# A state-space layer followed by a two-product MLP: the second product accumulated tile by tile, and the engine order written out by hand

## The chip, the cores and the metric

The kernel runs on one core of a Trainium2 chip. The metric is device time in microseconds (us), the median of several executions. One execution was recorded by the hardware profiler; its view is called the profile, and its rows the trace. The engines are PE (TensorE, with PEld for its weight loads), DVE (VectorE), ACT (ScalarE), POOL (GpSimd) and SP (SyncE, which here only issues DMAs).

## The reference

```python
# SSD part: batch 4, heads H=8, seq 768, head_dim 32, state 16; float32
cum   = cumsum(log(clip(a, 1e-6, 1)))                 # within a chunk
M     = (C @ B.T) * exp(cum_i - cum_j) * (i >= j)     # per head
y     = M @ x + exp(cum) * (C @ state)
state = exp(sum) * state + (B * exp(cum_last - cum)).T @ x
# MLP part: 3072 tokens, d_model 256, d_ff 2048; w_in and w_out arrive as float64
X = y.transpose(0, 2, 1, 3).reshape(3072, 256)
h = X @ w_in
g = maximum(h, 0) + alpha * minimum(h, 0)
out = g @ w_out
```

## The kernel before, in words

The sequence is cut into 24 chunks of Q = 128 tokens, and two chunks make a pair: 12 pairs, three to a batch element. Two pairs make a group of GT = 512 tokens, so there are NG = 6 groups of the MLP. The hidden width 2048 is NF = 16 tiles of 128.

`load_pair` fetches one pair's B and C (`nat`), x (`xt`), the decays in the layout of the states (`ap`), and the decays of all heads copied to every partition (`abc`, two transfers of 512 KB). `load_rows` and `rows_prep` make the products of the decays from a token to its chunk's end (`prt`) for two batch elements at a time.

`pair(gp)` does the SSD part of one pair. DVE scans `ap` to running products `pf` (L246, L249). POOL clips `abc` (L255), and DVE scans it, with an identity for each head (`ident_h`) as the added term, to the decay matrices `dec` (L258, 1024 elements a partition and chunk). PE transposes `nat` (L267); ACT copies B (`bh`, L271) and makes four masked copies of C (`cz`, L274); DVE makes `cd` (L276). POOL weights B (`bn`, L283), PE multiplies it with x (L290), and DVE masks the product and updates the state (`dm`, `state`, L292 and L302). PE forms the Gram matrices (L312), DVE multiplies them into `dec` (L317), PE sums state part and chunk part into `y` (L325, L332), and ACT copies `y` into the group's transposed input `xT` (L338).

`load_weights` brings a piece of a float64 weight (512 KB: two hidden tiles) as pairs of 32-bit words and builds float32 from them: on ACT `wt` and `wg` (L159, L164), on DVE a clip (L160), the sign, a shift with an exclusive or (L173), and an add (L176). The sign is taken by POOL for `w_in` (L167, 512 elements) and by DVE for `w_out` (L171, two of 256). There are eight pieces of each weight.

`hidden(g, q, t0, nt)` makes four hidden tiles: for each, PE sums two products into `hp` (L352; every float32 product is two matmul instructions in the trace, so four a tile), ACT scales by alpha (L355) and DVE takes the maximum (`gt`, L356). `hp` has two buffers (`ps_h`). `output(g)` then makes the second product: for each 128 tokens, 16 products summed into one `po` (L366, 32 instructions), a DVE copy (L368) and a store for each two.

The last lines set the program order: pair 0; then for group 0 the first 256 tokens with the pieces of `w_in`, and the last 256 with those of `w_out`, pairs 1 to 3 between; `output(0)`; then for each further group four calls of `hidden`, before two of which a pair of the next group is called, and `output(g)`. This is not the order in which the engines work: on every engine the order is set by a planner, which places each instruction by the times that it expects, and takes the program's order as priority. Within an engine's queue the planned order is then strict. Tiles from a pool of n buffers wait for the release of the tile n before.

Of the kernel before, what the change touches and what calls it, by code (L numbers as in the profile page):

```python
# [22 lines left out]
def kernel(  # L23
# [18 lines left out]
    nc = tc.nc  # L42

# [16 lines left out]
    FQ = 4  # L60
    WQ = 256
    assert H * N == P and HD == d_model and KC == 2 and R == CPB == 6
    assert NCH % GC == 0 and GT == 512 and NF % FQ == 0 and d_model <= WQ
# [5 lines left out]
    wld = ctx.enter_context(tc.tile_pool(name="wld", bufs=4))  # L69
    wtp = ctx.enter_context(tc.tile_pool(name="wtp", bufs=2))  # L70
    lda = ctx.enter_context(tc.tile_pool(name="lda", bufs=2))
# [3 lines left out]
    gp = ctx.enter_context(tc.tile_pool(name="gp", bufs=5))  # L75
# [14 lines left out]
    def load_pair(gp):  # L90
        b, c = divmod(2 * gp, CPB)
        sl = slice(c * Q, (c + 2) * Q)
        nat = ldx.tile([P, 2, 2, H * N], F32, name="nat")
        abc = lda.tile([P, 2, H * Q], F32, name="abc")
# [4 lines left out]
                                              ap=[[S, H], [0, N], [1, 2 * Q]]))  # L99
        for k in range(2):  # L100
# [5 lines left out]
        for k in range(2):  # L106
            ts = slice((c + k) * Q, (c + k + 1) * Q)
            first = a[b, 0:1, ts]
            nc.sync.dma_start(
                out=abc[:, k].rearrange("p (h t) -> p h t", h=H),  # L110
                in_=bass.AP(tensor=first.tensor, offset=first.offset, ap=[[0, P], [S, H], [1, Q]]),
            )
        for k in range(2):
            ts = slice((c + k) * Q, (c + k + 1) * Q)
            nc.sync.dma_start(out=xt[:, k].rearrange("p (h d) -> p h d", h=H),
                              in_=x[b, :, ts, :].rearrange("h p d -> p h d"))
# [19 lines left out]

    def load_weights(dst, src, sg):

        d = dst.bitcast(U32)
        if src.dtype == F32:
            nc.sync.dma_start(out=dst, in_=src)
            for i in range(2 if sg else 0):
# [3 lines left out]
        raw = wld.tile([P, 2, WQ, 2], U32, name="raw")  # L148
        nc.sync.dma_start(out=raw.rearrange("p k w t -> p k (w t)"), in_=src.bitcast(U32))
        hi = raw[:, :, :, 1]  # L150
        half = raw.rearrange("p k w t -> p k (w t)").bitcast(U16)
        half = half.rearrange("p k (w t) -> p k w t", t=4)[:, :, :, 1]
        t = wtp.tile([P, 2, WQ], U32, name="wt")
        r = wtp.tile([P, 2, WQ], U32, name="wr")
        g = wtp.tile([P, 2, WQ], F32, name="wg")
        tf = t.bitcast(F32)


        nc.scalar.activation(out=tf, in_=hi.bitcast(F32), func=ACTF.Abs, scale=0.125)  # L159
        nc.vector.tensor_scalar(out=tf, in0=tf, scalar1=F64_INF, scalar2=F64_ZERO,  # L160
                                op0=ALU.min, op1=ALU.max)


        nc.scalar.activation(out=g, in_=half, func=ACTF.Copy,  # L164
                             scale=2.0**-11, bias=2.0**25)
        if sg is None:
            nc.gpsimd.tensor_scalar(out=r, in0=hi.bitcast(F32), scalar1=0.0, scalar2=2.0**31,  # L167
                                    op0=ALU.is_lt, op1=ALU.mult)
        else:
            for i in range(2):  # L170
                nc.vector.tensor_scalar(out=r[:, i], in0=hi[:, i], scalar1=SIGN, scalar2=sg[i],  # L171
                                        op0=ALU.bitwise_and, op1=ALU.bitwise_xor)
        nc.vector.scalar_tensor_tensor(out=r, in0=t, scalar=3, in1=r,  # L173
# [8 lines left out]
    for h in range(H):  # L182
        nc.scalar.copy(out=ident_h[:, h * Q : (h + 1) * Q], in_=ident)
# [35 lines left out]
    prt = {}  # L219

    def rows_prep(i):
# [4 lines left out]
                                op0=ALU.max, op1=ALU.min)  # L226
        nc.vector.memset(d0[:, Q:], 0.0)
# [10 lines left out]
    def pair(gp):  # L238
# [3 lines left out]
        last = c + 2 == CPB  # L242


        pf = work.tile([P, 2 * Q], F32, name="pf")
        nc.vector.tensor_scalar(out=ap, in0=ap, scalar1=1e-6, scalar2=1.0, op0=ALU.max, op1=ALU.min)  # L246
        for k in range(2):
            ks = slice(k * Q, (k + 1) * Q)
            nc.vector.tensor_tensor_scan(out=pf[:, ks], data0=ap[:, ks], data1=zeros, initial=1.0,  # L249
                                         op0=ALU.mult, op1=ALU.add)  # L250


# [180 lines left out]
```

## Time and profile before

| | |
|---|---|
| median of 3 runs | 472.55 us (472.06 to 475.72) |
| the profiled execution's own time | 473.27 us |
| its span in the profile | 471.6 us |
| PE busy | 426.3 us, 1867 matmul instructions |
| DVE busy | 233.2 us |
| ACT busy | 120.1 us |
| POOL busy | 62.9 us |
| bytes moved by DMA | 32.38 MB |

Span and busy times come from the profiled execution; its own time is 1.67 us above its span, and 0.72 us above the median. A busy time is the time in which at least one instruction of the engine ran. The end of a matmul in the trace is modelled, so that PE counts as busy while it crawls at a low clock.

### The profile page before, as it was taken

The numbers are of one execution on the slowest core, as the hardware profiler recorded it, in microseconds if no ns is written. First come the engines' busy times: TensorE is split into PE (matmuls) and PEld (weight loads), VectorE is DVE, ScalarE is ACT, GpSimd is POOL, SyncE is SP. The second block draws the span as 40 slices with busy tenths as digits, with TensorE's granted clock in tenths as the row PEclk, the third lists the DMA queues.
The fourth block names the chain that finished last, engine by engine and source line by source line (L and its number), as shares of the span: only waits on it lengthen the run. The fifth ranks groups of instructions, "written<-read, shape, count | busy, mean of one in ns | idle before, by whom it ended". The sixth has DMA issues, their size and how long they took to land.

```text
span 471.6 us, 4815 instructions
## 1 busy us (share of the span) xinstructions
PE 426.3 (90%) x1867; PEld 271.4 (58%) x1867; DVE 233.2 (49%) x363; ACT 120.1 (25%) x225; POOL 62.9 (13%) x78
## 2 busy tenths in 40 slices
PE   1788679999989799998989998989999999999996
PEld 0345346658844358843448853448864458833785
DVE  2998779899584830065840065840043530034200
ACT  4135437610033220033330023330024320034100
POOL 3554450303401010011010000000000000000000
PEclk9868889999999999999999999999999999999999
DMA  9995668935643430034330030000000000000000
GB/s 166 229 200 201 154 169 188 197 53 136 181 78 90 56 89 1 22 64 105 45 90 1 23 56 12 1 0 0 24 22 0 1 0 24 0 22 1 0 22 22
DMA packets 109365, 32.38 MB, mean 69 GB/s; under 512 B 75856, under 2 KB 105248, under 8 KB 109344
## 3 DMA queue, kind: packets, MB, share of 16 engines
q1 hardware_dynamic: 105184, 31.83, 29.3%
q10 hardware_dynamic: 4160, 0.26, 0.6%
q8 instruction: 14, 0.23, 0.2%
q14 instruction: 7, 0.06, 0.0%
HBM read 28.94 MB, written 3.15 MB: 68 GB/s over the span
## 4 chain that ended last, share of the span: by engine, by line
PE 66%; DVE 15%; issue 9%; ACT 3%; DMA 3%; POOL 2%; SPq 0%; DVEq 0%; POOLq 0%; ACTq 0%
PE po L366 31%; PE hp L352 28%; DVE dec L258 5%; DVE gt L356 3%; PE ss L332 2%; DVE dec L317 2%; POOL wr L167 2%; PE ss L325 1%; DVE pf L249 1%; PE ss L312 1%; ACT gt L355 1%; ACT cz L274 1%; DMA ap<-in_a_dram 1%; PE ss L290 1%; DMA abc<-in_a_dram 1%
## 5 line engine op out<-in xcount | busy, mean ns | idle before, releaser
L352 PE MATMUL hp<-xT,w_in 128*128 128x512 f32 (+1 forms) x448 | 184.9, 560 | 20.1 <-DVE gt L356 18.1
L366 PE MATMUL po<-w_out,gt 128*128 128x256 f32 x768 | 168.9, 380 | 0.2 <-DVE o_sb L368 0.2
L366 PEld LDWEIGHTS po<-w_out,gt 128*128 128x128 f32 x768 | 145.6, 190 | 23.0 <-issue 3.0
L352 PEld LDWEIGHTS hp<-xT,w_in 128*128 128x128 f32 x448 | 81.9, 197 | 112.8 <-DVE gt L356 52.4
L356 DVE SCALAR_TENSOR_TENSOR gt<-hp,s_mul,gt 128x512 f32<-128x512 f32 (+1 forms) x112 | 74.2, 670 | 79.8 <-ACT gt L355 79.4
L355 ACT ACTIVATE gt<-hp,s_alpha 128x512 f32<-128x512 f32 (+1 forms) x112 | 70.0, 627 | 146.6 <-PE hp L352 146.4
L368 DVE COPY o_sb<-po 128x256 f32<-128x256 f32 x24 | 10.2, 423 | 124.6 <-PE po L366 124.6
L258 DVE TENSOR_TENSOR_SCAN dec<-abc,ident_h 128x1024 f32<-128x1024 f32 x24 | 55.4, 2331 | 3.3 <-PE ss L332 3.3
L255 POOL TENSOR_SCALAR abc<-abc 128x1024 f32<-128x1024 f32 x24 | 30.3, 1261 | 112.2 <-DMA abc<-in_a_dram 81.4
L312 PE MATMUL ss<-cz,bh 64*128 64x512 f32 x96 | 33.5, 695 | 6.1 <-DVE cd L276 4.1
L271 ACT COPY bh<-ss 128x256 f32<-128x256 f32 x12 | 4.4, 370 | 105.9 <-PE ss L267 105.9
L317 DVE TENSOR_TENSOR dec<-ss,dec 128x512 f32<-128x512 f32 x48 | 30.5, 680 | 0.6 <-PE ss L312 0.6
L283 POOL TENSOR_TENSOR bn<-nat,prt 128x256 f32<-128x256 f32 x12 | 10.4, 871 | 103.9 <-PE ss L290 56.7
L312 PEld LDWEIGHTS ss<-cz,bh 64*128 64x128 f32 x96 | 10.3, 203 | 22.7 <-ACT cz L274 7.7
L167 POOL TENSOR_SCALAR wr<-raw 128x512 uint32<-128x512 f32 x8 | 17.4, 2192 | 16.6 <-DVE w_in L176 12.9
L274 ACT ACTIVATE cz<-ss,par 128x256 f32<-128x256 f32 x48 | 19.4, 485 | 0.0
L332 PE MATMUL ss<-dec,xt 128*32 128x128 f32 x384 | 17.0, 292 | 2.2 <-DVE dec L317 2.2
L338 ACT COPY xT<-ss 128x512 f32<-128x512 f32 x12 | 7.0, 586 | 44.9 <-PE ss L332 44.9
L173 DVE SCALAR_TENSOR_TENSOR wr<-wt,wr 128x512 uint32<-128x512 uint32 x16 | 12.5, 787 | 5.0 <-POOL wr L167 5.0
L159 ACT ACTIVATE wt<-raw 128x512 f32<-128x512 f32 x16 | 10.7, 675 | 15.9 <-DMA raw<-in_moe_w_in_dram 10.9
L290 PE MATMUL ss<-xt,bn 128*128 128x256 f32 x40 | 12.0, 417 | 2.6 <-POOL abc L257 2.6
L332 PEld LDWEIGHTS ss<-dec,xt 128*32 128x32 f32 x384 | 9.6, 113 | 8.1 <-DVE dec L317 4.3
(46 smaller groups left out, 129.8 us busy)
## 6 DMA issues: line engine op xcount, KB each, us to landing
abc<-in_a_dram SPq DMA_DIRECT2D x24, 512.0 KB, 5.6
raw<-in_moe_w_in_dram SPq DMA_DIRECT2D x8, 512.0 KB, 6.1
raw<-in_moe_w_out_dram SPq DMA_DIRECT2D x8, 512.0 KB, 4.1
xt<-in_x_dram SPq DMA_DIRECT2D x24, 128.0 KB, 4.6
out_dram<-o_sb SPq DMA_DIRECT2D x12, 256.0 KB, 2.1
ap<-in_a_dram SPq DMA_DIRECT2D x12, 128.0 KB
nat<-in_B_dram SPq DMA_DIRECT2D x22, 64.0 KB, 2.8
nat<-in_C_dram SPq DMA_DIRECT2D x22, 64.0 KB, 2.7
```

Source lines behind the costliest of these rows:

```text
L167: nc.gpsimd.tensor_scalar(out=r, in0=hi.bitcast(F32), scalar1=0.0, scalar2=2.0**31, op0=ALU.is_lt, op1=ALU.mult)
L255: nc.gpsimd.tensor_scalar(out=abc[:, k], in0=abc[:, k], scalar1=1.0, scalar2=1e-6, op0=ALU.min, op1=ALU.max)
L258: nc.vector.tensor_tensor_scan(out=dec[:, k].rearrange("p h t -> p (h t)"), data0=abc[:, k], data1=ident_h, initial=0.0, op0=ALU.mult, op1 ...
L274: nc.scalar.mul(cz[:, e].rearrange("p k t -> p (k t)"), ct, par[:, e : e + 1])
L290: nc.tensor.matmul(dps[:, k * HD : (k + 1) * HD], bn[:, k], xt[:, k], start=True, stop=True)
L312: nc.tensor.matmul(gram[r].rearrange("p h t -> p (h t)"), bh[rs, k], cz[rs, :, k], start=True, stop=True, tile_position=(64 * r, 0), skip_ ...
L317: nc.vector.tensor_tensor(out=dec[:, k, hs], in0=gram[r], in1=dec[:, k, hs], op=ALU.mult)
L332: nc.tensor.matmul(y[32 * q : 32 * q + 32, w, k], xt[:, k, h * D : (h + 1) * D], dec[:, k, h], start=False, stop=True, tile_position=(0, 3 ...
L352: nc.tensor.matmul(hp, w_in[:, k, f * P : (f + 1) * P], xts[g][:, k, t0 : t0 + nt], start=(k == 0), stop=(k == KC - 1))
L355: nc.scalar.mul(gt, hp, s_alpha[:, f : f + 1])
L356: nc.vector.scalar_tensor_tensor(out=gt, in0=hp, scalar=s_mul[:, f : f + 1], in1=gt, op0=ALU.mult, op1=ALU.max)
L366: nc.tensor.matmul(po[:, :d_model], gts[g, f // FQ][:, f % FQ, ts], w_out[:, f], start=(f == 0), stop=(f == NF - 1))
```

## The change

The order of PE, DVE and ACT is now the program's order, instruction by instruction (`manual_schedule`); POOL and the DMA queues are still placed by the planner. With this, six things change:

- `hidden(g, f, ...)` makes one hidden tile, and `output(g, f)` adds that tile's share to all four 128-token blocks of the group at once, in two `po` tiles of 512 columns (8 matmul instructions of 256 columns). It follows the first product by LAG = 2 tiles. ACT, not DVE, copies `po` out (two copies of 512 columns a group).
- `pair` is a generator of six stages: loads, `bn`, `pf`, transposes and `cz`; the scan of the first chunk; the scan of the second, states; Gram matrices of the first chunk; of the second; `y`. In groups 1 to 4 the stages of a pair are called ahead of tiles 0, 1, 2, 3, 4 and 6 of each eight. In group 0 two tables (`first`, `second`) give the places.
- For pairs 0 and 1 `abc` isn't loaded: PE spreads the clipped rows (`firsts[0]`) over the partitions, by a product with a column of the identity, into PSUM, 512 columns at a time, and DVE scans from there. The buffers of `abc` are now three single chunks.
- The conversion of weights is cut in two: `convert_a` on ACT, `convert` on DVE. The sign of `w_in` is taken by DVE in one instruction, not by POOL. Transfers run six pieces ahead (`wld` has 6 buffers), the ACT part two pieces and the DVE part one piece ahead of the tiles that use them.
- The first transfers are put in the order pair 0, two weight pieces, pair 1, four pieces, pair 2.
- `ident_h` is made by one DVE copy instead of eight on ACT.

```diff
+    ctx.enter_context(tc.manual_schedule(engines={
+        mybir.EngineType.PE, mybir.EngineType.DVE, mybir.EngineType.Activation}))
...
+    LAG = 2
+    NB = 2
...
-    wld = ctx.enter_context(tc.tile_pool(name="wld", bufs=4))
+    wld = ctx.enter_context(tc.tile_pool(name="wld", bufs=6))
...
-    gp = ctx.enter_context(tc.tile_pool(name="gp", bufs=5))
+    gp = ctx.enter_context(tc.tile_pool(name="gp", bufs=16))
...
+        for k in range(2 if gp >= NB else 0):
+            t = lda.tile([P, H * Q], F32, name="abc")
...
+    def convert_a(dst, src, sg):
...
+        nc.scalar.activation(out=t.bitcast(F32), in_=hi.bitcast(F32), func=ACTF.Abs, scale=0.125)
+        nc.scalar.activation(out=g, in_=half, func=ACTF.Copy, scale=2.0**-11, bias=2.0**25)
...
         if sg is None:
-            nc.gpsimd.tensor_scalar(out=r, in0=hi.bitcast(F32), scalar1=0.0, scalar2=2.0**31,
-                                    op0=ALU.is_lt, op1=ALU.mult)
+            nc.vector.tensor_single_scalar(out=r, in_=hi, scalar=SIGN, op=ALU.bitwise_and)
...
+        for k in range(2):
+            if abc:
+                nc.vector.tensor_tensor_scan(out=dv[:, k], data0=abc[k], data1=ident_h,
+                                             initial=0.0, op0=ALU.mult, op1=ALU.add)
+            for w in range(0 if abc else 2):
+                t = ps_s.tile([P, 512], F32, name="ss")
+                for q in range(4):
+                    row = (b % 2 * H + 4 * w + q) * CPB + c + k
+                    nc.tensor.matmul(t[:, q * Q : (q + 1) * Q],
+                                     ident[:RW, row : row + 1].to_broadcast([RW, P]), firsts[0],
+                                     start=(q == 0), stop=True, skip_group_check=True)
+                nc.vector.tensor_tensor_scan(out=dv[:, k, ws], data0=t, data1=ident_h[:, ws],
+                                             initial=0.0, op0=ALU.mult, op1=ALU.add)
...
+    def output(g, f):
+
+        if f == 0:
+            pos[g] = [ps_o.tile([P, 2, d_model], F32, name="po") for i in range(GC // 2)]
+        gt = gts.pop((g, f))
+        for t in range(GC):
+            nc.tensor.matmul(pos[g][t // 2][:, t % 2], gt[:, t * Q : (t + 1) * Q], w_out[:, f],
+                             start=(f == 0 and t % 2 == 0), stop=(f == NF - 1),
+                             skip_group_check=True)
+        if f == NF - 1:
+            for i, po in enumerate(pos.pop(g)):
+                o_sb = op.tile([P, 2, d_model], F32, name="o_sb")
+                nc.scalar.copy(out=o_sb, in_=po)
...
+    pieces = in_pieces + out_pieces
+    for i in range(2):
+        load_weights(*pieces[i])
+    load_pair(1)
+    for i in range(2, 6):
+        load_weights(*pieces[i])
+    ssm(0, 5)
+    convert_a(*pieces[0])
+    convert(*pieces[0])
+    convert_a(*pieces[1])
     ssm(0)
+    load_pair(2)
+
+    first = {2: (1, 1), 3: (1, 1), 4: (1, 1), 6: (1, 1), 8: (1, 1), 10: (1, 1),
+             11: (2, 1), 12: (2, 1), 13: (2, 1), 15: (2, 1)}
+    second = {1: (2, 1), 3: (2, 1), 4: (3, 1), 6: (3, 1), 7: (3, 1), 9: (3, 1), 11: (3, 1), 13: (3, 1)}
+    for n in range(2):
+        for f in range(NF):
+            i = (n * NF + f) // 2
...
+            if f in (first, second)[n]:
+                ssm(*(first, second)[n][f])
+            hidden(0, f, n * 2 * Q, 2 * Q)
+            if f % 2 == 0 and i + 6 < len(pieces):
+                load_weights(*pieces[i + 6])
+            if f % 2 == 1 and i + 1 < len(pieces):
+                convert(*pieces[i + 1])
+                if i + 2 < len(pieces):
+                    convert_a(*pieces[i + 2])
+            if n and f >= LAG:
+                output(0, f - LAG)
+    for i in range(NF * (NG - 1) + LAG):
+        g, f = divmod(NF + i, NF)
+        nxt = 2 * g + 2 + f // 8
...
+        if f % 8 in (0, 1, 2, 3, 4, 6) and nxt < NP:
+            ssm(nxt)
+        if g < NG:
+            hidden(g, f, 0, GT)
+        output(*divmod(NF + i - LAG, NF))
```

More of the change, by code (lines that the diff above doesn't have):

```diff
@@ L181 @@
     ident_h = const.tile([P, H * Q], F32, name="ident_h")
-    for h in range(H):
-        nc.scalar.copy(out=ident_h[:, h * Q : (h + 1) * Q], in_=ident)
+    nc.vector.tensor_copy(out=ident_h.rearrange("p (h t) -> p h t", h=H),
+                          in_=ident.unsqueeze(1).to_broadcast([P, H, Q]))
     bmask = const.tile([P, HD], F32, name="bmask")
@@ L219 @@
     prt = {}
+    firsts = {}
     def rows_prep(i):
@@ L396 @@
-    output(0)
-    for g in range(1, NG):
-        for q in range(NQ):
-            if g + 1 < NG and q % 2 == 0:
-                ssm((g + 1) * GC // 2 + q // 2)
-            hidden(g, q, 0, GT)
-        output(g)
+            gts[g, f] = gp.tile([P, GT], F32, name="gt")
+        hp = ps_h.tile([P, GT], F32, name="hp")[:, :nt]
+        for k in range(KC):
+            nc.tensor.matmul(hp, w_in[:, k, f * P : (f + 1) * P], xts[g][:, k, t0 : t0 + nt],
+                             start=(k == 0), stop=(k == KC - 1))
```

171 lines of the change are left out of this document (82 added, 89 removed).

## The prediction, written before the changed kernel ran

> **What bounds the kernel now.** I read the page first: PE is busy 90% of the span and holds 66% of the chain that ended last, so what counts is where PE waits, and where it is busy without being at its rate.
>
> ```profile
> span 471.6 us, 4815 instructions
> ...
> PE 426.3 (90%) x1867; PEld 271.4 (58%) x1867; DVE 233.2 (49%) x363; ACT 120.1 (25%) x225; POOL 62.9 (13%) x78
> ...
> PEclk9868889999999999999999999999999999999999
> ...
> PE 66%; DVE 15%; issue 9%; ACT 3%; DMA 3%; POOL 2%; SPq 0%; DVEq 0%; POOLq 0%; ACTq 0%
> ```
>
> In the clock's row each digit is a slice of 11.8 us; in slices 2 to 6 it falls to 6 to 8 tenths. So I cut the span into stages (columns: length, then busy time and instructions of PE, PEld, DVE, ACT and POOL, the granted clock, the share of DMA and its rate).
>
> ```profile
> 0.00:30.00 30.00, 14.85 (x64) 7.78 (x64) 19.70 (x34) 9.62 (x24) 16.10 (x23) 0.88 0.94 194
> ...
> 30.00:72.00 42.00, 31.88 (x121) 17.97 (x120) 32.70 (x58) 18.82 (x37) 19.01 (x15) 0.80 0.66 177
> ...
> 72.00:122.00 50.00, 48.56 (x257) 35.90 (x258) 48.32 (x84) 17.76 (x37) 11.50 (x13) 1.00 0.69 151
> ...
> 122.00:174.00 52.00, 46.50 (x207) 24.13 (x207) 31.62 (x44) 15.05 (x27) 7.88 (x14) 1.00 0.43 96
> ...
> 201.60:246.00 44.40, 39.63 (x174) 17.87 (x173) 29.89 (x41) 15.05 (x27) 7.12 (x12) 1.00 0.40 80
> ...
> 344.80:384.30 39.50, 39.01 (x176) 17.97 (x175) 19.61 (x31) 15.04 (x27) 0.00 (x0) 1.00 0.02 7
> ```
>
> Up to 122 us DVE is the fuller engine (19.7 of 30, 32.7 of 42, 48.3 of 50), while PE lacks 15.2, 10.1 and 1.4 us of these stages, at a clock of 0.88, 0.80 and 1.00. From 122 on PE leads, but loses 5.5 us (122 to 174) and 4.8 (201.6 to 246) in the stages that hold pairs with their scans; where the last pairs run (344.8) it loses 0.5. The waits name the cause:
>
> ```profile
> PE hp L352 <- DVE gt L356: 18.1, 9, 4.1
> ...
> DVE wr L173 <- POOL wr L167: 5.0, 4, 1.9
> ```
>
> Two things, then: an opening bound by DVE and its partners, and DVE's scans that hold back `gt`, whose release the next `hp` needs. The rates of undisturbed PE come from the chain in order of time (start, length, what):
>
> ```profile
> 344.84 0.44 PE ss L267 x4
> ...
> 345.28 0.87 PE ss L290 x4
> ...
> 350.02 1.16 PE ss L325 x8
> ...
> 351.18 1.06 PE ss L332 x32
> ...
> 411.96 28.27 PE hp L352 x64
> ...
> 440.23 27.64 PE po L366 x128
> ...
> 467.90 0.42 DVE o_sb L368
> ```
>
> The second product, 128 instructions of 256 columns, takes 27.64 us: 0.216 each, without a gap. The first, 64 of 512 columns, takes 28.27, 0.442 each, where twice 0.216 would be 0.432: it waits a little for `gt` at every tile. A pair costs PE 0.44 (transposes), 0.87 (L290), 1.16 (L325), 1.06 (L332) and the Gram row, 1.99:
>
> ```profile
> 347.79 1.99 PE L312 MATMUL ss<-cz,bh 64*128 64x512 f32 x8
> ```
>
> together 5.52 us.
>
> **The change, groups 1 to 5.** A tile is 4 x 0.432 + 8 x 0.216 = 3.46 us of PE, and 80 tiles 276.4. Eight pairs (4 to 11) lie among them: 44.2. Two tiles of the lagging second product: 3.5. One transpose of decays: 0.4. Sum **324.5 us** if nothing waits. Does anything? The rows by form (busy us, mean ns; then idle before):
>
> ```profile
> L352 PE MATMUL hp<-xT,w_in 128*128 128x256 f32 x128 | 39.3, 448 | 9.9 <-DVE gt L356 7.9 <-DVE w_in L176 2.0
> ...
> L356 DVE SCALAR_TENSOR_TENSOR gt<-hp,s_mul,gt 128x512 f32<-128x512 f32 x80 | 59.3, 747 | 74.4 <-ACT gt L355 74.4
> ...
> L356 DVE SCALAR_TENSOR_TENSOR gt<-hp,s_mul,gt 128x256 f32<-128x256 f32 x32 | 14.9, 476 | 5.4 <-ACT gt L355 5.0
> ...
> L355 ACT ACTIVATE gt<-hp,s_alpha 128x512 f32<-128x512 f32 x80 | 55.0, 687 | 122.8 <-PE hp L352 122.8
> ...
> L355 ACT ACTIVATE gt<-hp,s_alpha 128x256 f32<-128x256 f32 x32 | 15.1, 476 | 23.8 <-PE hp L352 23.6
> ...
> L258 DVE TENSOR_TENSOR_SCAN dec<-abc,ident_h 128x1024 f32<-128x1024 f32 x24 | 55.4, 2331 | 3.3 <-PE ss L332 3.3
> ...
> L368 DVE COPY o_sb<-po 128x256 f32<-128x256 f32 x24 | 10.2, 423 | 124.6 <-PE po L366 124.6
> ...
> L160 DVE TENSOR_SCALAR wt<-wt 128x512 f32<-128x512 f32 x16 | 7.2, 467 | 0.0
> ...
> L171 DVE TENSOR_SCALAR wr<-raw,s_out 128x256 uint32<-128x256 uint32 x16 | 5.8, 395 | 0.0
> ...
> L173 DVE SCALAR_TENSOR_TENSOR wr<-wt,wr 128x512 uint32<-128x512 uint32 x16 | 12.5, 787 | 5.0 <-POOL wr L167 5.0
> ...
> L176 DVE CUSTOM_DVE_ANT_0 w_in<-wr,wg 128x1024 uint16<-128x1024 uint16 x8 | 6.8, 876 | 0.0
> ...
> L176 DVE CUSTOM_DVE_ANT_0 w_out<-wr,wg 128x1024 uint16<-128x1024 uint16 x8 | 5.6, 699 | 0.0
> ```
>
> After the first product of a tile come ACT 0.69 and DVE 0.75; the buffer of `hp` is wanted again only after two shares of the second product and one first product, 5.2 us, and `gt` itself 6.9 us later. In the worst stage DVE's queue holds one scan (2.33), a mask and two state updates (estimated from rows of their sizes, L173's 0.68 and two of L356's 0.48: 1.64) ahead of `gt`: 4.0 + 0.75 is done inside 5.2. ACT's `cz` stands ahead of one scaling only. Before, two scans stood back to back, and the buffer was wanted 1.73 us after. So the wait of 18.1 us should go. What is late next is PE itself. Bounds: 324.5, and 341 if each of the eight pairs still cost the 2.0 us that the nine waits of L352 average (16). ACT's two copies of `po` (1.2 to 1.4 us by L338 below and L355) stand between the last share of a group and the first of the next; there the first product of tile 2, 1.73 us, covers them. The 10.2 us of L368 leave DVE, where nobody waited for them except at the end. SP's queue gets a store behind each `po` copy; the loads behind it are those of a pair wanted eight tiles, 27 us, later.
>
> **The opening to the first tile.**
>
> ```profile
> 4.07 0.42 PE L267 MATMUL ss<-ident,nat 128*128 128x128 f32 x1
> ...
> 9.09 0.48 PE L267 MATMUL ss<-ident,nat 128*128 128x128 f32 x1 [1.66 <-DMA nat<-in_C_dram]
> ...
> 24.74 0.58 ACT L338 COPY xT<-ss 128x512 f32<-128x512 f32 x1 [1.17 <-PE ss L332]
> ...
> 26.89 1.63 POOL L283 TENSOR_TENSOR bn<-nat,prt 128x256 f32<-128x256 f32 x1
> ...
> 28.02 1.06 DVE L173 SCALAR_TENSOR_TENSOR wr<-wt,wr 128x512 uint32<-128x512 uint32 x1
> ...
> 29.93 0.68 DVE L173 SCALAR_TENSOR_TENSOR wr<-wt,wr 128x512 uint32<-128x512 uint32 x1
> ...
> 30.26 4.14 PE L352 MATMUL hp<-xT,w_in 128*128 128x256 f32 x8
> ```
>
> Before, the last transpose of pair 0 waits for its load until 9.09, `y` is copied at 24.74, and the first hidden matmul starts at 30.26, when DVE has converted a piece. Now 1 MB of `abc` is gone from the first transfers:
>
> ```profile
> abc<-in_a_dram SPq DMA_DIRECT2D x24, 512.0 KB, 5.6
> ```
>
> I put the transposes at 7 (bounds 4.5, where they would wait for the decays' transposes, and 9.1). Then 0.6 for them, one spread of four heads, eight matmuls of 128 columns like the eight of L325 (1.16), the pair's DVE work, and a conversion. DVE's pair: 233.2 in all, less 74.2 (both L356 forms), 10.2 (L368), 7.2 + 5.8 + 12.5 + 6.8 + 5.6 (conversions), is 110.9, over 12 pairs **9.2**. The half scans are taken as halves of L258 (1.17 each; PSUM as source isn't in the trace for a scan: bounds 1.1 and 1.5), the other seven spreads lie beside them. A conversion: L160 0.45, L173 0.68 undisturbed (29.93), L176 0.70, the sign 0.6 (one of 512 elements, between L160's 0.45 and two of L171, 0.72): **2.45**; by the means of the rows it would be 2.74, the upper bound. Sum 7 + 0.6 + 1.2 + 9.2 + 2.45 = 20.4, of which the `ap` part runs while `nat` is awaited: **20 us**. `ident_h` on DVE (two L160, 0.9, up to one L258, 2.3) and the rows' extra clip fall into the wait for loads; without it they would cost themselves.
>
> L173 took 1.06 us at 28.02, beside POOL's L283 of 26.89 to 28.52, and 0.68 alone. The Trainium skill (SBUF — State Buffer, "Who interferes with whom") says that a VectorE instruction with two SBUF inputs contends with a GpSimd instruction that reads SBUF; by that page every conversion would shed what POOL cost it, and the trace agrees in these two rows. Were the 1.06 kept, the first half below would be 8 x 0.38 = 3.0 us longer; its only POOL work now is `bn` and pair 2's clips, so I take 0.68.
>
> **First half of group 0** (16 tiles of 256 tokens, eight pieces of `w_in`, pair 1, and pair 2 to its first Gram stage). DVE: 16 x 0.466 + 8 x 2.45 + 9.2 + 7.9 = 44.1. Each tile's matmuls wait for their conversion, and DVE then waits for matmul and ACT unless a stage stands between. Four instructions of the 256-column row take 4 x 0.307 = 1.23 at the clock of this stage, ACT 0.47. Tiles 0, 10 and 14 have no DVE stage ahead: 1.8 each; 2, 6 and 8 are covered by 1.1 to 1.3: 0.6 each; three odd tiles wait 0.76 for their matmul: 9.5. Sum **53.6 us**. DVE's order here is strict: behind a conversion that waits for its words stand `gt`, and so `hp`, and PE. The words: pair 0, six pieces and pair 1 are 4.4 MB, at the 194 GB/s of the first row 23 us, and piece 5 is wanted at about 43.
>
> **Second half**: PE 16 x 0.864 + 14 x 1.73 = 38.0, pair 3 5.5, the rest of pair 2 3.2, and 1.3 while conversion and `gt` of the turn pass: **48 us**. DVE has 16 x 0.466 + 7 x 2.55 + 10.5 = 35.8, so it follows. **End**: before 3.7 us from the last matmul; now the second ACT copy, 0.58 to 0.69, for 0.42: **4**.
>
> 20 + 53.6 + 48 + 324.5 + 4 = 450.1 us of span, and 1.67 around it: 451.8 against 473.27. The median of the runs was 0.72 lower, so **451**. A check by place: groups 0 and 1 were done at 201.6, where the fifth stage above begins; now at 121.6 + 55.3 + 11 + 3.5 = 191.4. About 10 us come from the opening and 11 from later scans.
>
> **Rivals.** (1) *The clock.* PE is busy some 27 of 54 us in the first half, less than the 31.9 of 42 at which the clock row shows 0.80. At half clock the 1.23 becomes 1.73, in nine places: 4.5 us, **456**; PE's work would still fit beneath DVE's. The Trainium skill (TensorE: Matmul & The Clock Gate, "Part 1") says that about 3.4 us without PE work put the array back to half rate; by that page this rival is to be expected, while the trace shows 0.80 with idle times up to 4 us. (2) *The opening gains nothing*: the stages' hops between PE, ACT and DVE show, and it lasts 132 instead of 121.6: **462**. (3) *Fixed order loses, slower*: in the first 120 us DVE stands for each chain in turn, with nothing pulled ahead. A piece then costs 2.45 + 1.23 + 0.47 + 2 x 0.47 = 5.1, eight 41; pairs 1 and 2 each take what pair 0 took from 4.07 to 24.74 alone, 20: the first half 81, the second 62 with pair 3 bared, and the whole 494. It decides from an opening of 144 us on; the tables, which put DVE stages between conversion and `gt` at ten of 16 tiles, speak against it. (4) *Order without effect*: POOL and the queues are still planned, and loads planned late stop a strict DVE; what is won is waited away, **472**. (5) *Better*: few bare hops and conversions at 2.2: 438.
>
> **How the numbers follow.** Forecast 0.58 (445 to 460), clock 0.08, no gain in the opening 0.10, slower 0.10, no effect 0.07, better 0.07. One per cent, 4.7 us, is about what a measurement can tell from no change. Faster: 0.58 + 0.08 + 0.10 + 0.07 = 0.83; within 0.07; slower 0.10. The range 438 to 468 leaves out the slower, the no-effect and part of the better case; it holds the main stage's upper bound (341) with the rest as forecast.
>
> **What would show it.** The first hidden matmul near 20 us; DVE near full and PE half idle to about 74; from about 122 PE without a gap, chain pieces of L352 and L366 alternating at 1.73; no wait of `hp` for `gt` there; busy PE near 405 us. The prediction is wrong if DVE in the first half waits for DMA or PE more than 10 us in all, or if a pair in groups 1 to 4 costs over 6 us above its 27.6 us of tiles.

## The result, and the profile after

The changed kernel takes 456.27 us (median of 4 runs, 455.88 to 456.93) against 473.96 for the kernel before (four runs here, 472.06 to 475.72): a ratio of 0.9629, 95% interval 0.958 to 0.9678. It is 17.7 us faster; 451 was forecast, in a range of 438 to 468. Lines of the changed kernel have other numbers: the first product is L396, ACT's scaling L399, DVE's maximum L400, the second product L409.

The page of the kernel after, with the rows that answer to those of before:

```profile
span 455.2 us, 4968 instructions
...
PE 421.7 (93%) x1931; PEld 284.0 (62%) x1931; DVE 230.6 (51%) x354; ACT 124.3 (27%) x229; POOL 35.1 (8%) x62
...
PEclk9959787999999999999999999999999999999999
...
PE 86%; DVE 9%; DMA 1%; ACT 1%; issue 1%; ACTq 0%; DVEq 0%
```

PE's share of the chain rose from 66 to 86%, POOL's work fell from 62.9 to 35.1 us, and from the eighth slice on the clock stays at nine tenths or more. The span cut at the forecast's own stages (columns as before: length, busy time and instructions of PE, PEld, DVE, ACT, POOL, granted clock, DMA share, rate):

```profile
0.00:22.10 22.10, 13.11 (x87) 9.34 (x87) 14.55 (x32) 5.90 (x11) 3.67 (x12) 1.00 0.94 210
22.10:78.30 56.20, 36.81 (x162) 26.00 (x163) 39.58 (x68) 19.00 (x40) 8.13 (x13) 0.76 0.70 163
78.30:126.40 48.10, 47.29 (x275) 38.42 (x274) 36.89 (x74) 18.77 (x38) 3.25 (x5) 1.00 0.28 64
126.40:451.50 325.10, 324.53 (x1412) 210.23 (x1410) 139.61 (x182) 80.01 (x139) 20.10 (x32) 1.00 0.17 40
451.50:455.20 3.70, 0.00 (x0) 0.00 (x0) 0.00 (x0) 0.59 (x1) 0.00 (x0) 1.00 0.42 142
```

From 126.4 to 451.5 PE is idle for 0.6 us in 325: nothing is left there but PE's work. Nearly all the waiting is ahead of 78.3. In the stage from 22.1 to 78.3 neither PE (36.8 of 56.2) nor DVE (39.6) is full. PE's waits over the whole run (us in total, times, longest):

```profile
PE hp L396 <- DVE w_in L195: 21.3, 8, 5.3
...
PE hp L396 <- DVE gt L400: 0.8, 1, 0.8
```

The 18.1 us of waits of `hp` for `gt` are 0.8 now. In their place stand 21.3 us in which the first product waits for the conversion of its weights, at eight places, one for each piece of `w_in`. What DVE does in that stage is seen by its own waits from 22.1 to 78.3:

```profile
DVE gt L400 <- ACT gt L399: 13.2, 10, 2.7
DVE dec L322 <- PE ss L318: 1.1, 2, 0.7
DVE dec L361 <- PE ss L356: 1.0, 1, 1.0
```

So the two engines wait in turn. One turn, in the trace by time (start, length, engine, what, idle before and who ended it):

```profile
72.45 0.69 DVE L195 CUSTOM_DVE_ANT_0 w_in<-wr,wg 128x1024 uint16<-128x1024 uint16 x1
...
73.19 2.07 PE L396 MATMUL hp<-xT,w_in 128*128 128x256 f32 x4 [5.28 <-DVE w_in L195]
...
75.31 0.47 ACT L399 ACTIVATE gt<-hp,s_alpha 128x256 f32<-128x256 f32 x1 [5.77 <-PE hp L396]
75.81 0.48 DVE L400 SCALAR_TENSOR_TENSOR gt<-hp,s_mul,gt 128x256 f32<-128x256 f32 x1 [2.67 <-ACT gt L399]
```

PE had stood 5.28 us for this conversion; then DVE, whose next instruction in the fixed order is this tile's maximum, stands 2.67 us while matmul and scaling pass. Of this the four matmul instructions take 2.07 us; at 57.20, in the same stage, four of the same size take 1.13. The granted clock is 0.50 over the first and 1.00 over the second, so the low clock is part of this turn.

### The profile page after: what moved, and what is told of

It is laid out like the page before. It is cut to its first block, busy times and chain, and to the rows that moved or that the text cites. A ratio compares the mean times of both kernels' runs of the same rounds, so it can differ in the third digit from the quotient of the medians.

```text
span 455.2 us, 4968 instructions
## 1 busy us (share of the span) xinstructions
PE 421.7 (93%) x1931; PEld 284.0 (62%) x1931; DVE 230.6 (51%) x354; ACT 124.3 (27%) x229; POOL 35.1 (8%) x62
## 4 chain that ended last, share of the span: by engine, by line
PE 86%; DVE 9%; DMA 1%; ACT 1%; issue 1%; ACTq 0%; DVEq 0%
PE hp L396 37%; PE po L409 36%; PE ss L356 5%; PE ss L377 2%; PE ss L370 2%; PE ss L318 1%; PE ss L333 1%; DVE wr L192 1%; DMA nat<-in_C_dram 1%; DVE dec L322 1%; DVE gt L400 1%; DVE w_in L195 1%; DVE dec L312 1%; PE ss L296 1%; ACT gt L399 1%
## 5 line engine op out<-in xcount | busy, mean ns | idle before, releaser
L396 PE MATMUL hp<-xT,w_in 128*128 128x512 f32 (+1 forms) x448 | 192.4, 556 | 22.1 <-DVE w_in L195 21.3
L409 PE MATMUL po<-w_out,gt 128*128 128x256 f32 x768 | 181.1, 379 | 0.0
L409 PEld LDWEIGHTS po<-w_out,gt 128*128 128x128 f32 x768 | 145.9, 190 | 54.0 <-issue 38.3
L400 DVE SCALAR_TENSOR_TENSOR gt<-hp,s_mul,gt 128x512 f32<-128x512 f32 (+1 forms) x112 | 75.3, 673 | 186.9 <-ACT gt L399 186.0
L399 ACT ACTIVATE gt<-hp,s_alpha 128x512 f32<-128x512 f32 (+1 forms) x112 | 70.4, 629 | 263.7 <-PE hp L396 263.7
L396 PEld LDWEIGHTS hp<-xT,w_in 128*128 128x128 f32 x448 | 84.5, 198 | 89.3 <-issue 52.2
L312 DVE TENSOR_TENSOR_SCAN dec<-abc,ident_h 128x1024 f32<-128x1024 f32 x20 | 46.0, 2300 | 0.0
L272 POOL TENSOR_SCALAR abc<-abc 128x1024 f32<-128x1024 f32 x20 | 21.3, 1066 | 180.4 <-DMA abc<-in_a_dram 118.2
L356 PE MATMUL ss<-cz,bh 64*128 64x512 f32 x96 | 29.4, 682 | 0.0
L377 PE MATMUL ss<-dec,xt 128*32 128x128 f32 x384 | 13.3, 276 | 0.2 <-DVE dec L361 0.2
L322 DVE TENSOR_TENSOR_SCAN dec<-ss,ident_h 128x512 f32<-128x512 f32 x8 | 9.6, 1215 | 5.2 <-PE ss L318 5.2
L318 PEld LDWEIGHTS ss<-z,ident 96*128 96x128 f32 x64 | 11.4, 274 | 0.2
L318 PE MATMUL ss<-z,ident 96*128 96x128 f32 x64 | 11.3, 356 | 0.0
L166 ACT ACTIVATE wg<-raw 128x512 f32<-128x512 uint16 x16 | 10.8, 674 | 0.0
```

Of the source, the lines that this page charges most:

```text
L272: nc.gpsimd.tensor_scalar(out=t, in0=t, scalar1=1.0, scalar2=1e-6, op0=ALU.min, op1=ALU.max)
L312: nc.vector.tensor_tensor_scan(out=dv[:, k], data0=abc[k], data1=ident_h, initial=0.0, op0=ALU.mult, op1=ALU.add)
L318: nc.tensor.matmul(t[:, q * Q : (q + 1) * Q], ident[:RW, row : row + 1].to_broadcast([RW, P]), firsts[0], start=(q == 0), stop=True, skip_ ...
L356: nc.tensor.matmul(gram[r].rearrange("p h t -> p (h t)"), bh[rs, k], cz[rs, :, k], start=True, stop=True, tile_position=(64 * r, 0), skip_ ...
L377: nc.tensor.matmul(y[32 * q : 32 * q + 32, w, k], xt[:, k, h * D : (h + 1) * D], dec[:, k, h], start=False, stop=True, tile_position=(0, 3 ...
L396: nc.tensor.matmul(hp, w_in[:, k, f * P : (f + 1) * P], xts[g][:, k, t0 : t0 + nt], start=(k == 0), stop=(k == KC - 1))
```

## The experiments

Each is compared with runs of the kernel before on the same chip; between experiments the ratios are compared.

| kernel | median us | ratio to before | interval |
|---|---|---|---|
| after | 456.27 | 0.9629 | 0.958 to 0.9678 |
| before + interleaved second product | 461.13 | 0.971 | 0.9655 to 0.9765 |
| before + sign on DVE | 462.93 | 0.9794 | 0.9756 to 0.9832 |
| after, both scans at one tile | 456.23 | 0.9634 | 0.9582 to 0.9686 |
| after, a pair whole at one tile | 503.16 | 1.0614 | 1.0545 to 1.0683 |
| after, decays loaded | 461.45 | 0.9732 | 0.9684 to 0.9779 |
| after, idle PE filled | 460.52 | 0.9718 | 0.9693 to 0.9742 |
| after, planner's order | 442.82 | 0.9373 | 0.9323 to 0.9423 |
| after, conversions further ahead | 451.66 | 0.9553 | 0.9513 to 0.9592 |
| after, `w_in` in eight tiles | 454.7 | 0.9591 | 0.9562 to 0.962 |
| after, both of these | 444.39 | 0.9371 | 0.9329 to 0.9413 |
| planner's order, eight tiles | 443.7 | 0.9359 | 0.9311 to 0.9407 |
| both of these, first spread ahead | 442.69 | 0.934 | 0.9309 to 0.937 |

### What removed the wait for `gt`

First the interleaving alone, in the kernel before, with the planner's order, POOL's sign, loaded decays and pairs in one piece. `hidden` makes one tile instead of four, `output` adds one tile's share two tiles behind, and ACT copies `po` (heads of the functions and single lines only):

```diff
+    LAG = 2
...
-    gp = ctx.enter_context(tc.tile_pool(name="gp", bufs=5))
+    gp = ctx.enter_context(tc.tile_pool(name="gp", bufs=16))
...
-    def hidden(g, q, t0, nt):
+    def hidden(g, f, t0, nt):
...
-    def output(g):
+    def output(g, f):
...
+                nc.scalar.copy(out=o_sb, in_=po)
...
+        output(*divmod(NF + i - LAG, NF))
```

> The kernel before, planner and all, with one part of the change alone: the second product tile by tile, two tiles behind the first (and po copied by ACT). Theory A (in groups 1 to 5 the waits of PE for gt come from hp being wanted again after one tile, so the interleaving alone removes them): 11 us less from group 1 on, opening as before, 459 to 464. Theory B (the waits go only with stages placed by hand or with the other parts): 468 to 473.

Measured: 461.13 us, 13.0 below its before. In the chain of that kernel by time the two products alternate as in the kernel after:

```profile
138.20 1.72 PE hp L353 x4
139.92 1.73 PE po L366 x8
```

PE's waits from 130 us on (the same columns as above):

```profile
PE ss L326 <- DVE dec L318: 3.1, 8, 0.9
PE ss L333 <- DVE dec L318: 1.2, 3, 0.5
PE ss L313 <- DVE dm L293: 1.0, 1, 1.0
```

There is no row of `hp` waiting for `gt`. The interleaving does it by itself; neither the hand-written order nor the six stages are needed for that. What PE still waits for there is the pair's own parts, 5.3 us in these rows; in the kernel after PE is idle 0.6 us in its main stage. Then the other way round, with the interleaving kept and both scans of a pair again back to back:

```diff
-        if f % 8 in (0, 1, 2, 3, 4, 6) and nxt < NP:
-            ssm(nxt)
+        if f % 8 in (0, 2, 3, 4, 6) and nxt < NP:
+            ssm(nxt, 2 if f % 8 == 2 else 1)
```

> The changed kernel, with the two stages that hold a pair's scans called at one tile (tile 2 of eight) in groups 1 to 4. Theory A (the lag and the interleaving give 5.2 us before hp is wanted and 6.9 before gt is): DVE's queue then holds 6.3 us ahead of one gt, which is done 4.2 us after its matmul: no wait of PE, total as the changed kernel's within 1.5 us. Theory B (the spreading of scans over tiles is what took the waits away): about 2 us of PE waiting for each of eight pairs, as before, 16 us more: 472 us.

Measured: 456.23 us, no difference from the kernel after. PE's wait of `hp` for `gt`, whole run:

```profile
PE hp L396 <- DVE gt L400: 0.8, 1, 0.8
```

With two scans in a row the maximum of that tile ends 4.35 us after its matmul (140.90 less 136.55 in this run's trace; 4.2 was expected), inside the 5.2 us that the interleaving leaves. Last, all six stages at one tile, `if f % 8 == 0: ssm(nxt, 6)`:

> The changed kernel, with all six stages of a pair called at one tile (tile 0 of eight) in groups 1 to 4. Theory A (a fixed order has to be spread by hand, as PE then stands through a pair's whole chain on DVE and ACT): DVE's 10 us a pair lie bare but for PE's own 5.5 and one tile behind, 4 to 7 us more for each of eight pairs, 488 to 512 us in all. Theory B (slack of the lag and of PE's queue covers it): within 8 us of the changed kernel.

Measured: 503.16 us. Against the kernel after that is 46.9 us for eight pairs, 5.9 each, and the page's cause is not `gt`:

```profile
PE ss L356 <- DVE dm L335: 12.3, 8, 1.7
PE ss L356 <- ACT cz L303: 9.3, 8, 1.6
```

Waits of PE for the pair's own parts, each eight times, explain 21.6 of the 46.9 us in these two rows. Most of the rest is PE being busy for longer with the same number of instructions, 442.3 us where the kernel after has 421.7:

```profile
PE 442.3 (88%) x1931; PEld 295.3 (59%) x1931; DVE 226.9 (45%) x354; ACT 125.1 (25%) x229; POOL 42.4 (8%) x62
```

Behind the waits its instructions can run slowly: at 169.52 the eight of L370 take 2.07 us, at 131.88 in the same run 1.16, and the granted clock is 0.74 from 163 to 176 us and 1.00 from 128 to 134. In a strict order a pair's chain through PE, ACT and DVE is bare unless tiles stand between its stages. (That the planner lets a pair be called whole, in the interleaved kernel above, shows the same from the other side.)

### The opening: what won there

The sign of `w_in` on DVE, alone, in the kernel before:

```diff
-            nc.gpsimd.tensor_scalar(out=r, in0=hi.bitcast(F32), scalar1=0.0, scalar2=2.0**31,
-                                    op0=ALU.is_lt, op1=ALU.mult)
+            nc.vector.tensor_single_scalar(out=r, in_=hi, scalar=SIGN, op=ALU.bitwise_and)
```

> The kernel before, with one part of the change alone: the sign of w_in is taken by DVE (one instruction of 512 elements) in place of POOL. Theory A (POOL's 2.2 us instruction bounds each conversion in the opening, with DVE waiting 5.0 us for it and L173 slowed from 0.68 to 1.06 beside it): 4 to 8 us faster, 466 to 469 for a kernel before of 474. Theory B (the opening is held by something else, the planner's order or the loads): within 2 us of the kernel before.

Measured: 462.93 us, 9.3 below, more than was expected. The groups by form of the kernel before price the removed operation (busy us, mean ns):

```profile
L167 POOL TENSOR_SCALAR wr<-raw 128x512 uint32<-128x512 f32 x8 | 17.4, 2192 | 16.6 <-DVE w_in L176 12.9 <-DVE gt L356 1.9 <-DMA raw<-in_moe_w_in_dram 1.8
```

and those of the experiment the one put in its place:

```profile
L172 DVE SCALAR_TENSOR_TENSOR wr<-wt,wr 128x512 uint32<-128x512 uint32 x16 | 11.2, 698 | 0.0
...
L167 DVE TENSOR_SCALAR wr<-raw 128x512 uint32<-128x512 uint32 x8 | 3.3, 416 | 0.0
```

POOL took 2.19 us a time and DVE takes 0.42; the exclusive or behind it no longer waits (5.0 us before) and takes 0.698 instead of 0.787 us on average. Less the 3.3 us that DVE now spends on the sign itself, that is 5.0 + 1.4 - 3.3, some 3 us of the gain. The stages of 20 us, before:

```profile
20.00:40.00 20.00, 17.97 (x70) 9.85 (x69) 16.97 (x24) 6.28 (x14) 13.01 (x11) 0.60 0.89 241
40.00:60.00 20.00, 13.91 (x80) 7.91 (x80) 15.82 (x27) 12.03 (x24) 7.53 (x4) 0.91 0.58 152
```

and with the sign on DVE:

```profile
20.00:40.00 20.00, 17.42 (x118) 10.38 (x116) 20.00 (x32) 9.71 (x21) 5.71 (x7) 0.91 0.94 245
40.00:60.00 20.00, 14.11 (x48) 8.66 (x49) 19.55 (x40) 13.79 (x27) 2.88 (x3) 0.91 0.94 241
```

DVE went from 17.0 and 15.8 us of 20 to 20.0 and 19.6, and DMA's share in the second stage from 0.58 to 0.94: a POOL instruction in the middle of a DVE chain had stopped the pipeline of pieces. The other 6 us are put down to that, but it is not shown: the granted clock rose too, from 0.60 to 0.91 in the first of these stages, and no run splits the 6 us further.

Loading the first decays again, instead of spreading them by PE (`NB = 0`, four `abc` buffers in place of three):

> The changed kernel, with the decays of pairs 0 and 1 loaded and clipped by POOL as those of the other pairs, not spread by TensorE (abc has 4 buffers here). Theory A (the spread only trades a load of 2 MB for 64 matmuls on an idle, slow PE: the first tile starts at 22.1 either way, since the transposes wait for nat until 8.5 and scans could start near 10): within 3 us of the changed kernel, 453 to 459. Theory B (the 2 MB are what made the opening wait for loads): weights and pairs 2 and 3 come late, DVE waits in strict order, 5 to 10 us more, 461 to 466.

Measured: 461.45 us, a ratio 0.0103 above that of the kernel after, 4.9 us. That is beyond theory A and at the lower edge of theory B, but not by B's mechanism: up to 90 us the trace has no wait of DVE or PE's first product for a transfer. In its trace the first scan waits for POOL's clip of the loaded rows:

```profile
8.74 0.48 PE L296 MATMUL ss<-ident,nat 128*128 128x128 f32 x1 [1.37 <-DMA nat<-in_C_dram]
...
13.41 2.77 DVE L312 TENSOR_TENSOR_SCAN dec<-abc,ident_h 128x1024 f32<-128x1024 f32 x1 [6.37 <-POOL abc L274]
...
25.42 1.19 PE L396 MATMUL hp<-xT,w_in 128*128 128x256 f32 x2 [2.74 <-DVE w_in L195]
```

The spread wins 3.3 us by the first tile (25.42 against 22.09), because POOL leaves the path; most of the other 1.6 us is lost by tile 14, which starts 52.5 us after the first (77.93) instead of 51.1. `nat` is there at 8.74 with the 1 MB loaded and at 8.50 without: the transfer was not what `nat` waited for.

### The opening: what was lost there

The planner's order for the same program, that is, the two lines of `manual_schedule` left out:

> The changed program with its order left to the planner on PE, DVE and ACT too. Theory A (the new program, with the second product beside the first, leaves 5.2 us before a buffer of hp is wanted again, and that is what frees PE): PE still gapless in groups 1 to 4, total within 1% of the changed kernel's 456 us (452 to 461). Theory B (the strict order pays, since it keeps DVE's scans apart and the conversions in turn): scans stand together again or stages gather, PE waits for gt or dec about 2 us a pair in groups 1 to 4 (16 us) and the opening lengthens by some 5: 470 to 480 us.

Measured: 442.82 us, faster than either theory gave; the kernel after is 13.5 us behind it by the medians, 12.1 by the ratios. The stages:

```profile
20.00:40.00 20.00, 17.44 (x121) 12.96 (x118) 19.97 (x39) 9.16 (x19) 2.94 (x5) 1.00 0.90 237
40.00:60.00 20.00, 16.94 (x111) 10.81 (x110) 19.91 (x37) 10.59 (x22) 5.97 (x6) 0.94 0.89 202
...
112.20:436.50 324.30, 324.29 (x1412) 210.30 (x1410) 125.64 (x167) 79.94 (x139) 15.26 (x26) 1.00 0.15 33
```

The main stage lasts 324.3 us, as with the fixed order (325.1). All of the loss lies ahead of group 1, which starts at 112.2 instead of 126.4, although its first tile comes later (24.57 against 22.09). DVE is full. The planner pulls other work in where the fixed order waits.

Is it the clock? The kernel after has 0.76 in its first half. Sixteen unread matmul instructions behind every second tile of the first half keep PE busy:

```diff
+            if n == 0 and f % 2 == 1:
+                t = ps_s.tile([P, 512], F32, name="ss")
+                for i in range(8):
+                    nc.tensor.matmul(t[:, :256], ident, ident_h[:, :256], start=True, stop=True)
```

> The changed kernel with eight matmul instructions pairs of 256 columns, whose result nobody reads, behind every second tile of the first half of group 0 (64 products, 128 instructions, 28 us at full rate), to keep PE busy while it waits for conversions. Theory A (the low clock of 0.71 to 0.83 there costs some 4.5 us, as the first rival of the prediction had it): clock above 0.9, hidden matmuls near 0.9 us a tile in place of 1.0 to 2.1, total 450 to 454. Theory B (conversions and gt set the pace, the clock is a symptom): the filling delays tiles by as much as it wins, or more: 455 to 466.

Measured: 460.52 us, 4 more than the kernel after. Two stages of it, and then the trace at the end of the first half:

```profile
20.00:40.00 20.00, 17.93 (x110) 16.00 (x107) 15.76 (x26) 7.15 (x16) 3.22 (x5) 1.00 0.91 203
40.00:60.00 20.00, 20.00 (x123) 15.78 (x122) 12.85 (x26) 7.08 (x15) 1.79 (x3) 1.00 0.66 168
```

```profile
73.96 2.08 PE L396 MATMUL hp<-xT,w_in 128*128 128x256 f32 x4 [3.52 <-DVE w_in L195]
...
79.83 3.62 PE L462 MATMUL ss<-ident_h,ident 128*128 128x256 f32 x16
```

The clock is 1.00 from 20 to 60 us (the tile at 73.96 still crawls, 2.08 us), and yet tile 14 starts 51.4 us after the first (73.96 less 22.59), as in the kernel after (73.19 less 22.09, 51.1). The loss comes behind it, where the last filling, 3.62 us, stands bare ahead of tile 16.

This doesn't show that the low clock cost nothing. PE has no gap from 22.59 to 63.84 in this run, so the tiles there wait for the filling and no longer for the conversions. On the way the full clock did help: the conversion for tile 8 ends 26.9 us after the first tile (49.48 less 22.59), against 29.7 in the kernel after (51.83 less 22.09). Then filling and the matmuls of `y` stand ahead of tile 10, DVE waits 3.71 us for it (the maximum at 59.63), and the gain is gone. What a full clock would be worth without the filling stays open; 2.9 us is what was seen of it.

Is it the distance? One piece further ahead, conversion and ACT part alike:

```diff
     ssm(0)
+    convert(*pieces[1])
+    convert_a(*pieces[2])
...
-            if f % 2 == 1 and i + 1 < len(pieces):
-                convert(*pieces[i + 1])
-                if i + 2 < len(pieces):
-                    convert_a(*pieces[i + 2])
+            if f % 2 == 1 and i + 2 < len(pieces):
+                convert(*pieces[i + 2])
+                if i + 3 < len(pieces):
+                    convert_a(*pieces[i + 3])
```

> The changed kernel, with the conversions of both weights one piece further ahead of the tiles that use them (piece 1 right behind pair 0, then two pieces ahead). Theory A (in the first half of group 0 DVE and PE wait for each other in turn: PE idles 21 us for conversions, DVE some 14 for ACT's scaling): the matmuls of a tile run while DVE converts the next piece, the first half shrinks from 56 to 44 to 48 us, total 446 to 450. Theory B (DVE's own work or the low clock sets the first half): under 2 us gained, 454 to 456. Theory C (loads come too late for it): ACT waits for raw words, little gained.

Measured: 451.66 us, only 4.6 less (3.6 by the ratios, whose intervals overlap a little). The trace says why:

```profile
44.59 0.70 PE L396 MATMUL hp<-xT,w_in 128*128 128x256 f32 x2 [1.65 <-DVE gt L400]
...
46.99 0.69 DVE L195 CUSTOM_DVE_ANT_0 w_in<-wr,wg 128x1024 uint16<-128x1024 uint16 x1
...
47.74 2.93 PE L396 MATMUL hp<-xT,w_in 128*128 128x256 f32 x6 [2.45 <-DVE w_in L195]
```

A tile starts, makes two of its four instructions, and then waits 2.45 us for a conversion that ends at 47.68. By the program's order that is the piece after its own, which was ready at 40.26. The likely reason, which the next run tests: `w_in` is one tile of two halves (k = 0 and 1, each 2048 columns), and a piece writes 256 columns in both: the range from its first to its last word covers what lies between, the k = 1 columns of earlier pieces among it. So the matmul of k = 1 is held by the next piece. Eight tiles, one for each piece, would take that away:

```diff
-    w_in = const.tile([P, KC, d_ff], F32, name="w_in")
+    w_in = [const.tile([P, KC, WQ], F32, name=f"w_in{i}") for i in range(d_ff // WQ)]
...
-            nc.tensor.matmul(hp, w_in[:, k, f * P : (f + 1) * P], xts[g][:, k, t0 : t0 + nt],
+            nc.tensor.matmul(hp, w_in[f // 2][:, k, f % 2 * P : (f % 2 + 1) * P], xts[g][:, k, t0 : t0 + nt],
```

With both edits:

> The changed kernel with conversions one piece further ahead, as in the run before, and w_in held in eight tiles of 256 columns in place of one tile with both halves of d_model 2048 columns apart. Theory A (with one tile, the second half of each hidden tile's matmuls was made to wait for the later piece's conversion, as both spans overlap; with eight tiles it waits for its own alone): PE's waits for w_in in the first half fall from 8.6 us to under 2, DVE runs nearly full there, total 443 to 448. Theory B (the low clock or loads hold the first half): no more than 2 us off the 451.7 of the run before.

Measured: 444.39 us. The stages and the waits of PE from 20 to 85 us:

```profile
20.00:40.00 20.00, 14.19 (x69) 10.47 (x70) 19.37 (x33) 9.79 (x20) 3.57 (x5) 0.92 0.94 230
40.00:60.00 20.00, 15.26 (x86) 10.56 (x84) 19.15 (x33) 10.74 (x22) 2.65 (x4) 0.84 0.89 201
```

```profile
PE hp L396 <- DVE gt L400: 8.1, 5, 4.3
PE hp L396 <- DVE w_in L195: 1.9, 1, 1.9
```

DVE is full (19.4 and 19.2 of 20), the wait for conversions fell to 1.9 us, from 21.3 in the kernel after and 8.6 with the distance alone (there 3.7 more are put down to a load), and the fixed order is as fast as the planner's. The split alone:

> The changed kernel with w_in in eight tiles and nothing else. Theory A (the wait for a later piece exists only once conversions run further ahead; here the next tile needs the piece just converted anyway): no difference, 455 to 458. Theory B (the wait was there already): as much faster as the run with both, 444 to 448.

Measured: 454.7 us, no difference that the intervals show. (One of its four executions, the one with the trace, took 2448.8 us. The ratio is that of the other three, 453.74 to 454.87, and nothing is read from the trace.) And in the planner's order:

> The changed program with the planner's order on all engines, and w_in in eight tiles. Theory A (the planner too waited for later conversions): 2 to 4 us faster than with one tile, 438 to 441. Theory B (DVE is full in its opening, 19.9 of 20 us, so a freed PE changes nothing): within 1.5 us of 442.8.

Measured: 443.7 us, as without it: there DVE was full already. So the distance alone does little and the split alone nothing that shows, but the two together do it (after, distance, split, both): 0.9629, 0.9553, 0.9591 and 0.9371. Last, on top of both, pair 0's first spread ahead of its transposes:

> The version with conversions one piece further ahead and w_in in eight tiles, and pair 0's first chunk spread by TensorE ahead of the transposes, which wait for nat until 8.1. Theory A (DVE is full from its first scan at 10.7 to the first tile, so a scan 3 us earlier brings the first tile forward by 2 to 3.5 us, and the strict order passes that on): 440.5 to 442.5. Theory B (the chain through nat, cz and the Gram matrices sets the first tile): within 1 us of 444.4.

Measured: 442.69 us, the lowest of all, though its interval overlaps with those of the two above. The first tile is at 20.90 instead of 21.72.

## Why the prediction was right, and where not

**Groups 1 to 5: right.** 324.5 us forecast, 325.1 measured; a tile's two pieces take 1.72 and 1.73, 3.45 against 3.46, and group 2, with two pairs, lasts from 193.70 to 260.20, 66.5 (forecast 55.3 + 11 = 66.3). The reason was right too: the buffer is wanted two shares and one first product later. But what the check by place called "later scans" is the interleaving: two scans may stand together, as above. The scans' new places are worth nothing (0.9634 with both scans at one tile against 0.9629), and the interleaving alone gave 13.0 us.

**The check by place: wrong.** It put 10 us on the opening and 11 on later scans. Its mark, 201.6, stands behind group 1, so that it counted the waits of group 1 as opening. In the kernel before, the last shares of group 0 end, and pair 4 begins, at 128.89:

```profile
121.72 7.17 PE po L366 x32
128.89 0.44 PE ss L267 x4
```

In the kernel after pair 4 begins at 126.4, with two shares of group 0, 3.5 us, still to come. For equal work the opening lasts 129.9 us now and lasted 128.9: in this kernel it won nothing. All of the 16.4 us of span come from groups 1 to 5, which took 339.0 (128.9 to 467.9) and take 321.6 (325.1 less 3.5), 17.4 less. With the same marks the forecast was 3.8 from the opening (128.9 less 125.1, its 121.6 and the two shares) and 18.0 from the groups. So nearly the whole miss is in the opening.

**The opening to the first tile: 22.1 for 20.** The trace of the kernel after:

```profile
8.50 0.47 PE L296 MATMUL ss<-ident,nat 128*128 128x128 f32 x1 [0.99 <-DMA nat<-in_C_dram]
...
8.77 5.77 PE L318 MATMUL ss<-z,ident 96*128 96x128 f32 x32
...
10.72 1.22 DVE L322 TENSOR_TENSOR_SCAN dec<-ss,ident_h 128x512 f32<-128x512 f32 x1 [3.54 <-PE ss L318]
```

The term that was wrong is the 7 for the transposes: 8.5, within its bounds. The experiment with the decays loaded shows that their transfer had little to do with it (8.74 with it, 8.50 without). Spread and half scan were estimated at 1.2 and 1.17; the four spreads of this row took 5.77 together, 1.44 each, and the scan from PSUM 1.22, within its bounds.

**The first half: 56.2 for 53.6, by two errors that partly cancel.** DVE's work was put at 44.1 and is 39.6 busy: one of the eight conversions fell behind 78.3, and a conversion is cheaper than 2.45:

```profile
L192 DVE SCALAR_TENSOR_TENSOR wr<-wt,wr 128x512 uint32<-128x512 uint32 x16 | 11.1, 692 | 0.5
...
L190 DVE TENSOR_SCALAR wt<-wt 128x512 f32<-128x512 f32 x16 | 6.7, 420 | 0.0
...
L195 DVE CUSTOM_DVE_ANT_0 w_in<-wr,wg 128x1024 uint16<-128x1024 uint16 x8 | 5.8, 720 | 1.1
...
L184 DVE TENSOR_SCALAR wr<-raw 128x512 uint32<-128x512 uint32 x8 | 3.8, 474 | 0.0
```

0.692 + 0.420 + 0.720 + 0.474 is 2.31. The 0.68 taken for the exclusive or held for all 16, not only for the undisturbed ones. DVE's waits were put at 9.5 and are 56.2 less 39.6, 16.6, of which the rows above name 15.3. This is the term that failed. The prediction's own mark (more than 10 us of waits for DMA or PE) was passed, if ACT's scaling is counted with the matmul ahead of it; by the names in the rows alone PE released 2.1 us. "DVE near full" was wrong.

Turn by turn, the waits of the maximum in the trace were these. Tiles 0, 10 and 14, put at 1.8 each, took 1.79, 1.73 and 2.67. Tiles 2, 6 and 8, put at 0.6, took 1.70, 1.48 and 0.53. Tiles 1, 7, 9 and 11 took 1.03, 1.22, 0.38 and 0.71, for three of 0.76. The three that stand out, tiles 2, 6 and 14, are those whose four matmul instructions took 2.1 us, at a granted clock of 0.50, instead of the 1.23 of the sum. 2.9 of the 7.1 us are theirs. The 2.1 us of waits for spreads and Gram matrices had no term. That PE stands for the conversions meanwhile (21.3 us) the prediction had said; what it didn't ask is what a piece more of distance would change.

**The second half, 48.1 for 48, and the end, 3.7 for 4,** came out. "Busy PE near 405" did not: 421.7, and 36.8 of it in the first half, where a crawling PE counts as busy.

**The rivals.**

- *The clock*: its condition came (0.76), and its time, 456, is the one measured, but partly by luck. It priced 0.5 us at nine places; the trace has some 0.9 at three, the other misses lie elsewhere, and the run with filled PE could not price it. The Trainium skill (TensorE: Matmul & The Clock Gate, "Part 1") has idle PE fall back to half rate. The trace of the filled kernel agrees: up to 70.4 PE makes sixteen instructions in 3.62 us, then it stands 3.52 us, and the next four take 2.08 us, at a granted clock of 0.50, where four took 1.03 at 65.96.
- *The opening gains nothing* is what happened, by the marks above. Its 462 did not come, because its 132 us for the old opening also held the waits of group 1; by the right mark it would have been 125.4.
- *Fixed order loses* was right as a mechanism and wrong in size and sign: it costs 12 to 13 us against the planner with the same program, not the 43 between 451 and 494 (whose own terms add up to 492), and the opening ended at 126.4, not beyond the 144 from which it decides. The prediction made one case of the order and all that comes with it, and so didn't see that the rest of the change was worth about 30 us.
- *Order without effect* needed DVE to wait for loads; no wait of DVE for a transfer stands in its list.
- *Better* is what the program holds, 442.7 to 444.4, once little waits in the first half.

**Where the 17.7 us come from**, then: by place, all from groups 1 to 5. By part, the interleaving alone gave 13.0 and the sign alone 9.3, and all but the fixed order 29.4. If the two add up, which no run shows, some 7 us are left for spread, first transfers, `ident_h`, the distance of the loads and the stages; only the spread was measured (4.9, in the fixed order). The order takes back 12 to 13, and it does so in the opening: for equal work that lasts 115.7 us in the planner's order (112.2 + 3.5), 129.9 in the fixed one.

## What to carry to other kernels

When two engines are each two thirds busy in a stage and wait for one another at each turn, ask how far ahead the producer runs before asking what its instructions cost. An order written by hand needs that distance built in, which the planner found by itself here, and buffers whose writes don't overlap the reads that they are meant to run ahead of. And a change of many parts should be run with its order left to the planner as well: here the total was faster and hid an opening that lost some 13 us.

## What the runs showed of the hardware that was not expected

The sign of 512 words, read at every second word, took POOL 2.19 us, while its clip of 1024 contiguous words took 1.26 on average; DVE takes the sign in 0.42 with one bitwise instruction. Removing the eight was worth 9.3 us, more than half of their 17.4 us; DVE's chain waited behind them, 5.0 us by name. And the scan from PSUM costs hardly more for an element than the one from SBUF: 1.215 us for 512, 2.37 ns each, against 2.300 for 1024, 2.25 ns.
